# The first two tiles of x loaded turned, their means made on TensorE

## The chip, the cores and the metric

The kernel runs on one core of one Trainium2 chip. The metric is the device time of one execution in microseconds (us); the time of a kernel is the median of its runs.

## The reference

x is [1, 2048, 512] in fp32, 2048 tokens of 512 features. The output is a Fourier mixing of the normalized tokens, gated by an MLP on the same tokens, added to x:

```python
xn = _layernorm(x)                                   # over the 512 features, no weights
a  = einsum("bsd,ed->bse", xn, dft_hid_re)           # hidden DFT, 512 x 512
b  = einsum("bsd,ed->bse", xn, dft_hid_im)
s  = einsum("ts,bse->bte", dft_seq_re, a) - einsum("ts,bse->bte", dft_seq_im, b)
y  = _layernorm(xn)
h  = gelu(einsum("bsd,df->bsf", y, w1) + b1)         # 512 -> 1792
g  = silu(einsum("bsf,fd->bsd", h, w2) + b2)         # 1792 -> 512
out = x + s * g
```

## The kernel before

All products run on TensorE with fp32r operands: each fp32 operand is split into a rounded part (hi, an ACTIVATE copy on ScalarE) and the rest (lo, a subtraction on VectorE), and one product of whole values is taken as three: hi x hi, hi x lo and lo x hi. In `first_mm` a word such as "hl2" is one of these: the part of x, the part of the weight, and the feature chunk k of four.

The order of all instructions is written out by hand (`manual_schedule`); each engine runs its own in the order of the program and waits by semaphores. SP issues the loads in program order, and each waits for the landing of the eighth before it.

The hidden DFT comes first. Tokens are worked in tiles of 128, tiles 0 to 3 (the first 512 tokens) one by one. A product needs the feature axis on the partitions, for x as for the eight weight tiles W0 to W7 (four chunks k of the real matrix, m = 0, four of the imaginary, m = 1). `raw_w` are loaded by `load_w`, rounded by `round_w` (L356) and their rests made by `rest_w` (L81).

Tiles 2 and 3 are loaded twice: as rows (`x_load`, tile `x`), from which ScalarE makes minus the mean and the sum of squares (`first_mean`, `first_var`), and turned (`first_xT_load`, tile `xc`, features on the partitions). `first_transpose` brings the mean of each token to all partitions by one transpose (L311), VectorE adds it to the turned tile (L313), ScalarE rounds (L315), VectorE makes the rest (L316).

Tiles 0 and 1 are loaded as rows only. Tile 0's mean is made in two halves, one by ScalarE (L285), one by VectorE (L286, L287); VectorE centres the rows (L295), four transposes on TensorE turn them (L321), and two split steps per half tile (L62, L63) make hi and lo from PSUM. Tile 1 has its mean from ScalarE (L282), one centring (L291), four transposes and one split. Their squares are summed later on ScalarE from the centred tile (L302).

`idle_mm` issues products of a zero tile (L202) that nothing reads. `stats` makes mean and variance of tiles 4 to 7 on VectorE; `m_pack` (L171) packs their four means, `m_turn` (L179) turns them on TensorE. Tiles 4 to 7 are loaded turned, as one block of 512 tokens (`xt_load(1)`, L329), and centred at L334. `first_factors` (L141) makes the scale factors of tiles 0 to 7, by which ScalarE scales the products out of PSUM (`dft_out`, L431).

After this opening come the sequence DFT and the MLP, some 640 us of products, which the change doesn't touch.

Of the kernel before, what the change touches and what calls it, by code (L numbers as in the profile page):

```python
# [14 lines left out]
P = 128  # L15
# [5 lines left out]
def fnet_mixer_kernel(ctx: ExitStack, tc: tile.TileContext, x, xT, ct, wt, w1, w2, b1, b2, out):  # L21
# [118 lines left out]
    def first_factors():  # L140
        nc.vector.tensor_scalar(mv1[:, 2:NC, 1], mv1[:, 2:NC, 1], 1.0 / D, None, op0=ALU.mult)  # L141
        v = small.tile([P, 2 * HB], F32, tag="v", name="v")
        inner(v[:, :HB], mv1[:, :HB, 1], 1.0)
        outer(v[:, HB:], mv1[:, :HB, 1], 1.0)
        finish = rsqrt(rr[:, :2 * HB], v, 2 * HB)

        def both_signs():
            finish()
            nc.vector.tensor_scalar(nr1, rr[:, :HB], -1.0, None, op0=ALU.mult)

        return both_signs
# [52 lines left out]
    idle_mm(8)  # L204
# [10 lines left out]

    def parts(i):
        return 1 if i else 2
# [23 lines left out]
    x_load(0)  # L241
    for n in range(3):
        load_w(n)
    x_load(1)
    for n in range(3, 2 * NK):
        load_w(n)
    first_xT = {}

    def first_xT_load(i):
        first_xT[i] = plain(f"xc{i}").rearrange("p (k t) -> p k t", k=NK)  # L250
        nc.sync.dma_start(out=first_xT[i], in_=xT[TB[0], :, :, i * P:(i + 1) * P].rearrange("k p t -> p k t"))

    for i, load in ((4, x_load), (2, x_load), (5, x_load), (2, first_xT_load), (6, x_load), (3, x_load), (7, x_load),
                    (3, first_xT_load)):
        load(i)
# [6 lines left out]
    xc = {}  # L262

    half_means = [nr1[:, q:q + 1] for q in range(2)]
# [11 lines left out]
    def first_mean(i):  # L276
        if i > 1:
            nc.scalar.activation(junk(0), xs[i], AF.Copy, scale=-1.0 / D, accum_out=minus_mean(i))
            return
        xc[i] = plain(f"xc{i}")  # L280
        if i:
            nc.scalar.activation(xc[i], xs[i], AF.Copy, scale=1.0 / D, accum_out=mv1[:, i, 0:1])  # L282
            return
        n = D // 2
        nc.scalar.activation(xc[i][:, :n], xs[i][:, :n], AF.Copy, scale=1.0 / D, accum_out=half_means[0])  # L285
        nc.vector.reduce_sum(half_means[1], xs[i][:, n:], axis=mybir.AxisListType.X)  # L286
        nc.vector.tensor_scalar(half_means[1], half_means[1], 1.0 / D, None, op0=ALU.mult)  # L287

    def first_centre(i):
        if i:  # L290
            nc.vector.tensor_scalar(xc[i], xs[i], mv1[:, i, 0:1], None, op0=ALU.subtract)  # L291
            return
        n = D // 2
        for q in range(2):
            nc.vector.tensor_scalar(xc[i][:, q * n:(q + 1) * n], xs[i][:, q * n:(q + 1) * n], half_means[0],  # L295
                                    half_means[1], op0=ALU.subtract, op1=ALU.subtract)

    def first_var(i):
        if i > 1:
            nc.scalar.activation(junk(1), xs[i], AF.Square, bias=minus_mean(i), accum_out=mv1[:, i, 1:2])  # L300
            return
        nc.scalar.activation(xs[i], xc[i], AF.Square, scale=D ** -0.5, accum_out=mv1[:, i, 1:2])  # L302

    def first_transpose(i):
        t = operand(f"xt{i}")
        hi, lo = t[:, 0, :], t[:, 1, :]
        for k in range(NK):
            xt[i, k] = (hi[:, k * P:(k + 1) * P], lo[:, k * P:(k + 1) * P])
        if i > 1:
            pt = bank(f"pt{i}")  # L310
            nc.tensor.transpose(pt[:, :P], minus_mean(i).broadcast_to([P, P]), ident)  # L311
            c = first_xT[i]
            nc.vector.tensor_add(c, c, pt[:, None, :P].broadcast_to([P, NK, P]))  # L313
            c = c.rearrange("p k t -> p (k t)")
            nc.scalar.activation(hi, c, AF.Copy)  # L315
            return lambda: nc.vector.tensor_sub(lo, c, hi.bitcast(F32))  # L316
        n = D // parts(i)
        for q in range(parts(i)):
            pt = bank(f"pt{i}{q}")
            for k in range(NK // parts(i)):  # L320
                nc.tensor.transpose(pt[:, k * P:(k + 1) * P], xc[i][:, q * n + k * P:q * n + (k + 1) * P], ident)  # L321
            split_into(hi[:, q * n:(q + 1) * n], lo[:, q * n:(q + 1) * n], pt[:, :n])
# [125 lines left out]

    first_mean(0)
    first_centre(0)  # L450
    make_w(0)
    first_transpose(0)
    idle_mm(1)
    make_w(1, 2)
    first_mean(1)
    first_centre(1)
    make_w(3, 4)
    first_mm(0, 0, "hh0 hl0 lh0 hh1 lh1 hl1 hh2 lh2 hl2 hh3 lh3")
    first_transpose(1)
    first_mm(0, 0, "hl3")  # L460
    make_w(5, 6, 7)
    xt_load(1)
    for q in (12, 13, 8, 9):
        x_load(q)

    first_mm(0, 1, "hh0 lh0 hl0")
    first_mm(1, 0, "hh0 hl0 hh1 hl1 hh2 hl2 hh3 hl3 lh0 lh1 lh2 lh3")
    first_mean(2)
    first_var(0)
# [13 lines left out]
    nc.vector.tensor_add(mv1[:, 0, 0:1], *half_means)  # L483
# [225 lines left out]
    neg_means(0, 2)  # L709
# [690 lines left out]
```

## Time and profile before

| | us |
|---|---|
| median of 3 runs | 665.17 (664.75 to 665.47) |
| profiled execution | 665.25 |
| its span, first to last instruction | 663.5 |
| TensorE busy in the span | 658.4 |

The span begins with the first instruction and ends with the last; the 1.75 us of the profiled execution around it belong to its start and end. In rows, PE is TensorE's products, PEld its weight loads, ACT ScalarE, DVE VectorE, SP the engine that issues loads. "x4" merges four instructions that follow each other; the time given is then from the start of the first to the end of the last. A product's end lies behind the start of the next one, since products are pipelined: where the spacing of a series is wanted, the duration of one is to be taken off first. "idle before" says what the engine waited for.

### The profile page before, as it was taken

The numbers are of one execution on the slowest core, as the hardware profiler recorded it, in microseconds if no ns is written. First come the engines' busy times: TensorE is split into PE (matmuls) and PEld (weight loads), VectorE is DVE, ScalarE is ACT, GpSimd is POOL, SyncE is SP. The second block draws the span as 40 slices with busy tenths as digits, with TensorE's granted clock in tenths as the row PEclk, the third lists the DMA queues.
The fourth block names the chain that finished last, engine by engine and source line by source line (L and its number), as shares of the span: only waits on it lengthen the run. The fifth ranks groups of instructions, "written<-read, shape, count | busy, mean of one in ns | idle before, by whom it ended". The sixth has DMA issues, their size and how long they took to land.

```text
span 663.5 us, 8214 instructions
## 1 busy us (share of the span) xinstructions
PE 658.4 (99%) x2913; PEld 542.7 (82%) x2913; DVE 543.4 (82%) x584; ACT 361.0 (54%) x419; POOL 50.8 (8%) x84
## 2 busy tenths in 40 slices
PE   9999999999999999999999999999999999999997
PEld 5888888888888888888888888888888888888886
DVE  6899977877776866888979998739877299998986
ACT  6875567544446754555455544456444455746540
POOL 0002000321121100000000000000000001210100
PEclk9999999999999999999999999999999999999999
DMA  9979540987979999798699996416544558997984
GB/s 319 301 250 251 175 150 1 354 312 255 356 298 363 415 411 356 266 381 318 243 387 410 393 316 233 153 54 198 185 156 129 126 133 262 303 257 252 301 257 139
DMA packets 71869, 172.82 MB, mean 260 GB/s; under 512 B 6880, under 2 KB 22804, under 8 KB 71828
## 3 DMA queue, kind: packets, MB, share of 16 engines
q1 hardware_dynamic: 59488, 132.27, 56.9%
q0 software_dynamic: 12032, 39.86, 19.1%
q8 instruction: 23, 0.38, 0.2%
q10 hardware_dynamic: 308, 0.16, 0.1%
q14 instruction: 18, 0.15, 0.1%
HBM read 121.91 MB, written 50.36 MB: 260 GB/s over the span
## 4 chain that ended last, share of the span: by engine, by line
PE 99%; DMA 0%; DVE 0%; issue 0%; DVEq 0%
PE pz L1013 20%; PE px L1013 18%; PE ma L1013 11%; PE hy L828 11%; PE mb L1013 9%; PE hz L828 6%; PE pw L1013 5%; PE pd L408 3%; PE q1y L656 3%; PE hx L828 3%; PE pd L420 2%; PE px L1334 2%; PE pw L1334 2%; PE q1z L656 2%; PE quy L656 1%; PE q1x L656 1%
## 5 line engine op out<-in xcount | busy, mean ns | idle before, releaser
L1119 DVE TENSOR_TENSOR c<-c,c 128x1024 f32<-128x1024 f32 x32 | 39.1, 1222 | 3.4 <-DMA c<-ct 3.4
L81 DVE TENSOR_TENSOR w1l<-w1r,w1h 128x1792 fp32r<-128x1792 f32 x7 | 14.2, 2025 | 20.9 <-ACT w1h L527 20.9
L833 ACT ACTIVATE hc<-hc,b_t 128x1024 f32<-128x1024 f32 (+1 forms) x18 | 17.3, 962 | 25.1 <-DVE hc L873 22.6
L63 DVE TENSOR_TENSOR R_b1l<-c,R_b1h 128x1024 fp32r<-128x1024 f32 x16 | 19.5, 1221 | 13.0 <-ACT R_b1h L62 9.7
L62 ACT ACTIVATE R_s3h<-c 128x1024 fp32r<-128x1024 f32 x16 | 17.0, 1062 | 23.9 <-DVE c L1119 10.2
L1013 PE MATMUL pw<-R_s1h,L 128*128 128x512 f32 x96 | 29.7, 389 | 0.0
L62 ACT ACTIVATE R_b2h<-c 128x1024 fp32r<-128x1024 f32 x16 | 16.9, 1059 | 21.1 <-DVE c L1124 16.4
L63 DVE TENSOR_TENSOR R_s2l<-c,R_s2h 128x1024 fp32r<-128x1024 f32 x16 | 19.6, 1222 | 8.6 <-PE pz L1013 8.6
L62 ACT ACTIVATE R_s2h<-c 128x1024 fp32r<-128x1024 f32 x16 | 17.0, 1062 | 16.7 <-PE px L1013 9.3
L63 DVE TENSOR_TENSOR R_s3l<-c,R_s3h 128x1024 fp32r<-128x1024 f32 x16 | 19.6, 1224 | 3.9 <-PE pz L1013 3.8
L62 ACT ACTIVATE R_s1h<-c 128x1024 fp32r<-128x1024 f32 x16 | 16.4, 1052 | 11.3 <-DVE c L1130 11.3
L1127 POOL DMA_DIRECT2D c<-ct x8 | 7.0, 873 | 200.4 <-DVE c L1124 162.9
L62 ACT ACTIVATE R_b1h<-c 128x1024 fp32r<-128x1024 f32 x16 | 16.7, 1055 | 9.6 <-PE px L1013 4.4
L62 ACT ACTIVATE R_a1h<-c 128x1024 fp32r<-128x1024 f32 x16 | 16.9, 1055 | 8.9 <-PE pz L1013 7.2
L1013 PEld LDWEIGHTS pw<-R_s1h,L 128*128 128x128 f32 x96 | 18.0, 188 | 3.7
L63 DVE TENSOR_TENSOR R_b2l<-c,R_b2h 128x1024 fp32r<-128x1024 f32 x16 | 19.4, 1219 | 1.5 <-PE px L1013 1.5
L63 DVE TENSOR_TENSOR R_a1l<-c,R_a1h 128x1024 fp32r<-128x1024 f32 x16 | 19.5, 1221 | 1.3 <-PE px L1013 1.1
L63 DVE TENSOR_TENSOR R_s4l<-c,R_s4h 128x1024 fp32r<-128x1024 f32 x16 | 19.6, 1224 | 0.7 <-PE px L1013 0.7
L1124 DVE TENSOR_TENSOR c<-c,c 128x1024 f32<-128x1024 f32 x16 | 19.6, 1223 | 0.4
L62 ACT ACTIVATE R_s4h<-c 128x1024 fp32r<-128x1024 f32 x16 | 16.8, 1050 | 5.1 <-PE pz L1013 4.9
L63 DVE TENSOR_TENSOR R_s1l<-c,R_s1h 128x1024 fp32r<-128x1024 f32 x16 | 18.9, 1220 | 0.4 <-ACT R_s1h L62 0.2
L1013 PE MATMUL pw<-R_s1l,L 128*128 128x512 f32 x48 | 18.7, 389 | 0.0
(1000 smaller groups left out, 2221.4 us busy)
## 6 DMA issues: line engine op xcount, KB each, us to landing
c<-ct SPq DMA_DIRECT2D x68, 512.0 KB, 5.8
m<-h_d SPq DMA_DIRECT2D x48, 512.0 KB, 7.1
h_d<-ht POOLq DMA_DIRECT2D x21, 512.0 KB, 6.4
s_d<-sa SPq DMA_DIRECT2D x32, 256.0 KB, 3.7
la<-s_d SPq DMA_DIRECT2D x32, 256.0 KB, 5.7
h_d<-hc POOLq DMA_DIRECT2D x13, 512.0 KB, 3.7
x<-x SPq DMA_DIRECT2D x16, 256.0 KB, 5.6
sa<-a_d SPq DMA_DIRECT2D x8, 512.0 KB, 6.5
```

The source lines that it names most:

```text
L62: nc.scalar.activation(hi, src, AF.Copy)
L63: nc.vector.tensor_sub(lo, src, hi.bitcast(F32))
L81: nc.vector.tensor_sub(hi_lo[1], src, hi_lo[0].bitcast(F32))
L408: nc.tensor.matmul(acc, xt[i, k][px], weights[m * NK + k][pw], start=n == 0, stop=n == len(terms) - 1)
L420: nc.tensor.matmul(dacc[i, m], xt[i, k][px], weights[m * NK + k][pw], start=seen[i, m] == 0, stop=seen[i, m] == 3 * NK - 1)
L656: nc.tensor.matmul(qx[key], a, w, start=p in (1, 5, 2) and n == 0, stop=p in (2, 3, 4) and n == len(terms) - 1, skip_group_check=True)
L828: nc.tensor.matmul(acc[:, tau, :], w[:, W1_AT[p], k * P:(k + 1) * P], r[:, k, :], start=p in (1, 5, 2) and i == 0, stop=p in (2, 3, 4) and ...
L833: nc.scalar.activation(dst, src, AF.Gelu_apprx_tanh, bias=b1_t[:, row:row + 1])
L1013: nc.tensor.matmul(acc[k][:, tau, :], a, c[:, tau, :], start=first and i == 0, stop=last and i == len(terms) - 1, skip_group_check=True)
L1119: nc.vector.tensor_sub(t, t, raw)
L1124: nc.vector.tensor_add(raw, raw, t)
L1334: nc.tensor.matmul(acc[KEY[name]][k][:, tau, cols], a[k], c[:, tau, cols], start=False, stop=last and u == us[-1] and i == 2, skip_group_c ...
```

## The change

A new input `xf` holds the first 512 tokens turned, tile by tile (feature chunk, 128 tokens). Tiles 0 and 1 are loaded from it, in the places of SP's queue where their rows were loaded; the turned tiles 2 and 3 come from it too, in rows of 2 KB where there were four of 512 bytes. The mean of each token is made by TensorE: four fp32 products per tile with a matrix `per_d` whose values are all 1/512 sum a tile over its features and leave the mean in every partition. VectorE subtracts it, tile 0 in two halves and tile 1 in one, ScalarE rounds, VectorE makes the rests. The eight transposes of tiles 0 and 1 go, as do the sums that made their means. The rows of tiles 0 and 1 are loaded later, after those of tiles 4 and 2, and their means and squares are made from them on ScalarE, as for tiles 2 and 3. The idle products at the start are 5 and 2 in place of 8 and 1. Some orders change: the first products of tile 0 are split in two batches around tile 1's mean, tile 1's products come before the three of (0, 1), and the rows 12, 8 and 9 are loaded before the turned block of tiles 4 to 7.

```diff
@@ -138,7 +138,7 @@
         nc.vector.tensor_scalar(dst, var, scale * (1.0 + EPS), EPS * EPS, op0=ALU.mult, op1=ALU.add)
 
     def first_factors():
-        nc.vector.tensor_scalar(mv1[:, 2:NC, 1], mv1[:, 2:NC, 1], 1.0 / D, None, op0=ALU.mult)
+        nc.vector.tensor_scalar(mv1[:, :NC, 1], mv1[:, :NC, 1], 1.0 / D, None, op0=ALU.mult)
         v = small.tile([P, 2 * HB], F32, tag="v", name="v")
         inner(v[:, :HB], mv1[:, :HB, 1], 1.0)
         outer(v[:, HB:], mv1[:, :HB, 1], 1.0)
@@ -201,7 +201,10 @@
         for q in range(n):
             nc.tensor.matmul(idle_ps, idle[:, :P], idle, start=True, stop=True)
 
-    idle_mm(8)
+    per_d = consts.tile([P, P], F32, name="per_d")
+    nc.vector.memset(per_d, 1.0 / D)
+
+    idle_mm(5)
 
     xs = {}
 
...
@@ -238,20 +238,20 @@
     nc.scalar.activation(warm, warm, AF.Sqrt)
     nc.scalar.dma_start(out=touched[:P // 8].rearrange("p (n w) -> p n w", w=4),
                         in_=wt[:, :, 0:P:8, 0:4].rearrange("m k p w -> p (m k) w"))
-    x_load(0)
+    first_xT = {}
+
+    def first_xT_load(i):
+        first_xT[i] = plain(f"xc{i}").rearrange("p (k t) -> p k t", k=NK)
+        nc.sync.dma_start(out=first_xT[i], in_=xf[i])
+
+    first_xT_load(0)
     for n in range(3):
         load_w(n)
-    x_load(1)
+    first_xT_load(1)
     for n in range(3, 2 * NK):
         load_w(n)
-    first_xT = {}
-
-    def first_xT_load(i):
-        first_xT[i] = plain(f"xc{i}").rearrange("p (k t) -> p k t", k=NK)
-        nc.sync.dma_start(out=first_xT[i], in_=xT[TB[0], :, :, i * P:(i + 1) * P].rearrange("k p t -> p k t"))
-
-    for i, load in ((4, x_load), (2, x_load), (5, x_load), (2, first_xT_load), (6, x_load), (3, x_load), (7, x_load),
-                    (3, first_xT_load)):
+    for i, load in ((4, x_load), (2, x_load), (0, x_load), (1, x_load), (5, x_load), (2, first_xT_load), (6, x_load),
+                    (3, x_load), (7, x_load), (3, first_xT_load)):
         load(i)
     a_d = [dram.tile([2, P, D], F32, name=f"a_d{i}") for i in range(NS // 2)]
     b_d = [dram.tile([2, P, D], F32, name=f"b_d{i}") for i in range(NS // 2)]
...
@@ -274,52 +271,42 @@
         return nm[:, 2 * NC + i:2 * NC + i + 1]
 
     def first_mean(i):
...
+        nc.scalar.activation(junk(0), xs[i], AF.Copy, scale=-1.0 / D, accum_out=minus_mean(i))
 
     def first_var(i):
...
+        nc.scalar.activation(junk(1), xs[i], AF.Square, bias=minus_mean(i), accum_out=mv1[:, i, 1:2])
+
+    early_mean = {}
+
+    def mean_over(i):
+        early_mean[i] = bank(f"pm{i}")
+        for k in range(NK):
+            nc.tensor.matmul(early_mean[i][:, :P], per_d, first_xT[i][:, k, :], start=k == 0, stop=k == NK - 1)
+
+    def centre_first(i, ks):
+        c = first_xT[i][:, ks, :]
+        nc.vector.tensor_sub(c, c, early_mean[i][:, None, :P].broadcast_to([P, c.shape[1], P]))
+
+    first_op = {}
+
+    def first_round(i, ks):
+        if i not in first_op:
+            t = first_op[i] = operand(f"xt{i}").rearrange("p a (k t) -> p a k t", k=NK)
+            for k in range(NK):
+                xt[i, k] = (t[:, 0, k, :], t[:, 1, k, :])
+        nc.scalar.activation(first_op[i][:, 0, ks, :], first_xT[i][:, ks, :], AF.Copy)
+
+    def first_rest(i, ks):
+        hi, lo = (first_op[i][:, q, ks, :] for q in range(2))
+        nc.vector.tensor_sub(lo, first_xT[i][:, ks, :], hi.bitcast(F32))
 
     def first_transpose(i):
...
+        pt = bank(f"pt{i}")
+        nc.tensor.transpose(pt[:, :P], minus_mean(i).broadcast_to([P, P]), ident)
+        c = first_xT[i]
+        nc.vector.tensor_add(c, c, pt[:, None, :P].broadcast_to([P, NK, P]))
+        first_round(i, slice(0, NK))
+        return lambda: first_rest(i, slice(0, NK))
@@ -446,27 +433,43 @@
             round_w(n)
             rest_w(n)
 
+    front, back, whole = slice(0, 2), slice(2, NK), slice(0, NK)
+    mean_over(0)
+    idle_mm(2)
+    centre_first(0, front)
+    centre_first(0, back)
+    round_w(0)
+    first_round(0, front)
+    round_w(1)
+    first_round(0, back)
+    round_w(2)
+    first_rest(0, front)
+    rest_w(0)
+    first_rest(0, back)
+    rest_w(1)
+    rest_w(2)
+    first_mm(0, 0, "hh0 lh0 hh1 lh1 hl0")
+    mean_over(1)
+    centre_first(1, whole)
+    round_w(3)
+    round_w(4)
+    first_round(1, whole)
+    rest_w(3)
+    first_rest(1, whole)
+    rest_w(4)
+    first_mm(0, 0, "hh2 lh2 hl1 hh3 lh3 hl2 hl3")
+    make_w(5, 6, 7)
+    for q in (12, 8, 9):
+        x_load(q)
+    xt_load(1)
+    x_load(13)
+
+    first_mm(1, 0, "hh0 hl0 hh1 hl1 hh2 hl2 hh3 hl3 lh0 lh1 lh2 lh3")
+    first_mm(0, 1, "hh0 lh0 hl0")
+    first_mean(2)
     first_mean(0)
-    first_centre(0)
-    make_w(0)
-    first_transpose(0)
-    idle_mm(1)
-    make_w(1, 2)
+    first_var(0)
     first_mean(1)
-    first_centre(1)
-    make_w(3, 4)
-    first_mm(0, 0, "hh0 hl0 lh0 hh1 lh1 hl1 hh2 lh2 hl2 hh3 lh3")
-    first_transpose(1)
-    first_mm(0, 0, "hl3")
-    make_w(5, 6, 7)
-    xt_load(1)
-    for q in (12, 13, 8, 9):
-        x_load(q)
-
-    first_mm(0, 1, "hh0 lh0 hl0")
-    first_mm(1, 0, "hh0 hl0 hh1 hl1 hh2 hl2 hh3 hl3 lh0 lh1 lh2 lh3")
-    first_mean(2)
-    first_var(0)
     first_var(1)
     stats(mv1, xs[NC], NC)
     stats(mv1, xs[NC + 1], NC + 1)
@@ -480,7 +483,6 @@
     rest_2()
     stats(mv1, xs[NC + 3], NC + 3)
     m_pack()
-    nc.vector.tensor_add(mv1[:, 0, 0:1], *half_means)
     first_mm(1, 1, "hh0 hh1 hh2 hh3 lh0 lh1 lh2 lh3 hl0 hl1 hl2 hl3")
 
     def means_out():
@@ -706,7 +708,6 @@
     for q in (10, 11):
         stats(mv1, xs[q], q)
     neg_means(2)
-    neg_means(0, 2)
     a_sum(7)
     dft_mm(3, 0)
     dft_mm(3, 1)
@@ -1381,6 +1382,7 @@
     arrays = {
         "x": a["A_x"][0],
         "xT": a["A_x"][0].T.reshape(D // P, P, S // W, W).transpose(2, 0, 1, 3),
+        "xf": a["A_x"][0, :W].T.reshape(D // P, P, W // P, P).transpose(2, 1, 0, 3),
         "ct": np.stack([seq_halves(a["A_dft_seq_re"]), seq_halves(a["A_dft_seq_im"])]),
         "wt": np.stack([a[n].T.reshape(D // P, P, D) for n in ("A_dft_hid_re", "A_dft_hid_im")]),
         "w1": a["B_w1"].reshape(2, 2, P, 2, F // P // 2, P).transpose(4, 2, 3, 0, 1, 5).reshape(
```

## Rows read from the trace of the kernel before

**Rows 1.** The page, part 1: busy us, share of the span, instructions.

```profile
PE 658.4 (99%) x2913; PEld 542.7 (82%) x2913; DVE 543.4 (82%) x584; ACT 361.0 (54%) x419; POOL 50.8 (8%) x84
```

**Rows 2.** Chain of waits in order of time: start us, us, what.

```profile
0.75 2.93 DMA x<-x
...
4.98 1.09 PE pt L321 x4
6.06 0.43 PE idle_ps L202
6.49 2.97 PE pd L420 x11
9.89 5.06 PE pd L420 x22
...
72.01 16.32 PE q1y L656 x72
```

**Rows 3.** Timeline, all engines, 14 to 25 us: start, us, what, [idle before].

```profile
14.80 0.27 PE L311 MATMUL pt<-ident,fm 128*128 128x128 f32 x1
...
18.05 0.17 DVE L171 COPY rsm<-mv 128x4 f32<-128x4 f32 x1
...
18.33 0.08 PEld L179 LDWEIGHTS rpm<-ident,rsm 128*4 128x4 f32 x1 [0.24 <-issue]
...
24.50 2.35 DVE L334 TENSOR_TENSOR xT<-xT,rowm 128x1024 f32<-128x1024 f32 x2
```

**Rows 4.** Timeline of PE, 0 to 12 us.

```profile
1.20 3.60 PE L202 MATMUL idle_ps<-idle 128*128 128x512 bf16 x8 [1.20 <-DVE warm L237]
4.98 1.09 PE L321 MATMUL pt<-ident,xc 128*128 128x128 f32 x4 [0.18 <-DVE xc L295]
5.86 0.63 PE L202 MATMUL idle_ps<-idle 128*128 128x512 bf16 x1
6.11 3.35 PE L420 MATMUL pd<-W,xt 128*128 128x512 f32 x11
9.30 0.60 PE L321 MATMUL pt<-ident,xc 128*128 128x128 f32 x4
```

**Rows 5.** Two windows: busy us by engine, PEclk, DMA share, GB/s.

```profile
4.50:5.00 0.50, 0.32 (x2) 0.05 (x1) 0.50 (x2) 0.50 (x1) 0.00 (x0) 1.00 1.04 389
...
9.00:10.00 1.00, 1.00 (x8) 0.82 (x8) 0.99 (x2) 0.26 (x2) 0.00 (x0) 1.00 0.99 369
```

**Rows 6.** Loads issued at 2.62, 3.09, 7.67, 11.70 us: size, us to landing.

```profile
x<-x SPq DMA_DIRECT2D x1, 256.0 KB, 4.4
...
rw<-wt SPq DMA_DIRECT2D x1, 256.0 KB, 4.6
...
xc<-xT SPq DMA_DIRECT2D x1, 256.0 KB, 5.6
...
xT<-xT SPq DMA_DIRECT2D x1, 512.0 KB, 7.2
```

**Rows 7.** Timeline of PE near the end: first and last of seven products.

```profile
658.11 0.28 PE L1334 MATMUL px<-R_b1l,L 128*128 128x224 f32 x1
...
658.77 0.28 PE L1334 MATMUL px<-R_b1l,L 128*128 128x224 f32 x1
```

**Rows 8.** Timeline of ScalarE (ACT) and VectorE (DVE), 3.5 to 8 us.

```profile
5.67 0.81 ACT L62 ACTIVATE xt<-pt 128x256 fp32r<-128x256 f32 x2 [0.62 <-PE pt L321]
6.09 0.85 DVE L63 TENSOR_TENSOR xt<-pt,xt 128x256 fp32r<-128x256 f32 x2 [0.31 <-ACT xt L62]
6.38 1.14 ACT L356 ACTIVATE W<-rw 128x512 fp32r<-128x512 f32 x2
...
7.04 1.29 DVE L81 TENSOR_TENSOR W<-rw,W 128x512 fp32r<-128x512 f32 x2
```

**Rows 9.** Timeline of VectorE and ScalarE, 12 to 16 us.

```profile
15.10 0.69 DVE L313 TENSOR_TENSOR xc<-xc,pt 128x512 f32<-128x512 f32 x1 [0.43 <-PE pt L311]
...
15.83 0.63 ACT L315 ACTIVATE xt<-xc 128x512 fp32r<-128x512 f32 x1 [1.90 <-DVE xc L313]
```

More of the change, by code (lines that the diff above doesn't have):

```diff
@@ L20, in fnet_mixer_kernel @@
 @with_exitstack
-def fnet_mixer_kernel(ctx: ExitStack, tc: tile.TileContext, x, xT, ct, wt, w1, w2, b1, b2, out):
+def fnet_mixer_kernel(ctx: ExitStack, tc: tile.TileContext, x, xT, xf, ct, wt, w1, w2, b1, b2, out):
     nc = tc.nc
@@ L213, in tok @@
         return TB[i // NC] * NC + i % NC
-    def parts(i):
-        return 1 if i else 2
     def x_load(i):
@@ L240, in fnet_mixer_kernel @@
                         in_=wt[:, :, 0:P:8, 0:4].rearrange("m k p w -> p (m k) w"))
-    x_load(0)
-    for n in range(3):
-        load_w(n)
-    x_load(1)
-    for n in range(3, 2 * NK):
-        load_w(n)
     first_xT = {}
@@ L250, in first_xT_load @@
         first_xT[i] = plain(f"xc{i}").rearrange("p (k t) -> p k t", k=NK)
-        nc.sync.dma_start(out=first_xT[i], in_=xT[TB[0], :, :, i * P:(i + 1) * P].rearrange("k p t -> p k t"))
-    for i, load in ((4, x_load), (2, x_load), (5, x_load), (2, first_xT_load), (6, x_load), (3, x_load), (7, x_load),
-                    (3, first_xT_load)):
+        nc.sync.dma_start(out=first_xT[i], in_=xf[i])
+    first_xT_load(0)
+    for n in range(3):
+        load_w(n)
+    first_xT_load(1)
+    for n in range(3, 2 * NK):
+        load_w(n)
+    for i, load in ((4, x_load), (2, x_load), (0, x_load), (1, x_load), (5, x_load), (2, first_xT_load), (6, x_load),
+                    (3, x_load), (7, x_load), (3, first_xT_load)):
         load(i)
@@ L261, in fnet_mixer_kernel @@
     xt = {}
-    xc = {}
-    half_means = [nr1[:, q:q + 1] for q in range(2)]
     squares = []
@@ L276, in first_mean @@
     def first_mean(i):
[L277 to L296, printed above, removed]
-    def first_var(i):
[L299 to L302, printed above, removed]
@@ L304, in first_transpose @@
-    def first_transpose(i):
[L305 to L322, printed above, removed]
+        nc.scalar.activation(junk(0), xs[i], AF.Copy, scale=-1.0 / D, accum_out=minus_mean(i))
```

## The prediction, made before the changed kernel ran

> **What bounds the kernel now.** The page's first part comes first: TensorE (PE) is busy for 99% of the span [rows 1], so a change shows in the time only if it lengthens or shortens PE's own stream. The chain of waits says where that stream isn't yet closed: it runs through a load, VectorE and TensorE up to about 15 us, and from there through products that stand 0.227 us apart (72 in 16.32 us) with nothing between them [rows 2]. The change lies wholly in that opening. The point to watch is the transpose for tile 2, which starts at 14.80 [rows 3] after 4 + 4 transposes and 33 products: from there on the two kernels issue the same products in the same order, so the change is worth the shift of that one instruction, plus whatever arrives late behind it.
>
> The opening has two levels of speed. Four transposes of 128 columns take 1.09 us at 4.98, and the same four 0.60 us at 9.30; with the durations of the last one taken off (0.42, 0.27) they stand 0.22 and 0.11 us apart. Eight idle products of 512 columns stand 0.43 us apart, later ones 0.23 [rows 2, 4]. The granted clock reads 1.00 in both stretches [rows 5], but the spacings say that TensorE ran at 1.2 GHz until a little after 6 us and at 2.4 GHz from then on. The first mean falls in the slow part, the second in the fast one.
>
> **The change, part by part.** *Loads.* The first turned tile takes the place of the first row tile in SP's queue, with the same 256 KB, and lands at 0.75 + 2.93 = 3.68 [rows 2]. The second lands where row tile 1 did, at 2.62 + 4.4 = 7.0 [rows 6]. The early weights keep their places, and with them their landings (weight 3 at 3.09 + 4.6 = 7.7, weight 5 at 8.9).
>
> *Price of one fp32 product.* No row shows one. The lower end is the transpose of the same shape, 0.22 us at the slow level and 0.11 at the fast one. What bounds that row is probably its weights, for products of 224 columns stand just as far apart (seven starts, six intervals in 0.66 us: 0.11) [rows 7]: 128 or 224 columns, the spacing doesn't change. The upper end is a 512-column product with a load of weights that nothing hides: 0.43 + 0.22 = 0.65, at the fast level 0.34. I take 0.43 and 0.23, the rows of the 512-column product, the nearest to the middle between the ends. One pass over 128 columns is not likely to be all: for whole fp32 values the kernel itself takes three products of rounded parts (hh, hl, lh).
>
> *Tile 0.* Five idle products end their issue at 1.20 + 5 x 0.43 = 3.35, before the load lands. Products start at 3.72, the last at 3.72 + 3 x 0.43 = 5.01, its result at 5.64, 0.63 later, as long as the idle product at 5.86 takes [rows 4]. VectorE centres the front half in 0.42 (half-tile subtractions, 0.85 for two with overlap) [rows 8], 5.68 to 6.10. ScalarE, which has rounded weight 0 at 4.42 as before, rounds it in 0.38 [rows 8], 6.13 to 6.51. The two idle products end at 6.3 and cost nothing: behind them PE waits anyway. First weights at 6.56, and with 0.11 for that load the first product at 6.67; before it was 6.11 [rows 4]. This step costs 0.56: reduction, centring, transposes and rounding (3.68 to 6.06) give way to products, centring and rounding (3.68 to 6.51).
>
> *From there to the transpose of tile 2.* ScalarE: weight 1 6.41 to 7.03, back half to 7.32, weights 2, 3, 4 to 7.84, 8.36 and 8.93 (0.62 each, 0.52 apart: two in 1.14) [rows 8]. VectorE: back half centred by 6.45; rests of front half to 6.97, weight 0 to 7.58, back half to 7.92, weight 1 to 8.53, weight 2 to 9.14 (0.69 each, 0.60 apart, halves 0.42). PE: hh0 to 6.90; lh0 waits for 6.97 and runs 7.14 to 7.37; hh1, lh1, hl0 to 8.06; the second mean, 4 x 0.23, to 8.98, its result at 9.15; six products to 10.36. Meanwhile VectorE centres tile 1 from 9.19 to 9.88 (0.69, the row of a 512-element subtraction with a PSUM operand) [rows 9]; the rest of weight 3 is queued behind it and ends at 10.49, and ScalarE rounds tile 1 by 10.54. So the last product of that batch, hl3, stalls: 10.66 to 10.89. Then 12 + 3 + 6 products without a wait (rest of tile 1 at 11.3, of weight 4 at 11.9, weights 5 to 7 rounded at 11.1 to 12.1): 21 x 0.227 = 4.76, and the transpose starts at 15.65 against 14.80.
>
> As a sum: first product +0.56; second mean 0.92 in place of four transposes 0.44, +0.48; stalls now 14.80 - 6.11 - 33 x 0.227 - 0.44 = 0.76, then 0.58, -0.18. Together **+0.86 us**.
>
> *What is moved behind it.* The rows of tiles 0 and 1 come after those of 4 and 2, 0.5 MB in front of all later loads; at 0.66 us per 256 KB (weight 3 to weight 5: 7.7 to 8.9, two loads) each later landing moves by 1.3 us: the turned tile 2 from 7.67 + 5.6 = 13.3 to 14.6 [rows 6], needed at 15.97. The turned block for tiles 4 to 7 also has three row tiles in front of it now (12, 8, 9): it lands 1.3 + 2.0 us later than its 11.7 + 7.2 = 18.9 [rows 6], at 22.2, and is wanted at 24.50 + 0.86 [rows 3]. ScalarE gets two more sums of 0.62 + 0.19 us, in a stretch in which it sat idle for 1.90 us [rows 9]: from 12.0 on its three sums and two variances end at 12.0 + 0.61 + 2 x 1.46 = 15.5, before the rounding of tile 2 at 16.7. Tiles 2 and 3 turned come in rows of 2 KB, which can only help their landings. VectorE loses the half-tile reduction and three one-column operations. The narrowest point is the packing of four means at 18.05, whose transpose loads weights at 18.33 [rows 3]: VectorE's rests end some 0.6 us later than before, its packing at 19.1, PE gets there at 19.2. All this I cost at nothing; with the cover gone, PE would stand by the amount the packing is late.
>
> **Forecast.** The profiled execution took 665.25 us (span 663.5 and 1.75 around it), the median is 665.17, 0.08 less. 665.17 + 0.86 = **666.0 us**, within the 0.2% (1.3 us) that a measurement of this kernel can tell.
>
> **Rivals.** *Weights not hidden (slower).* If each fp32 product waits for its own weights, 0.65 and 0.34 apart, the first mean ends 0.66 + 0.2 later and the second 0.44 later: 0.86 + 0.86 + 0.3 to 0.44 = +2.1, **667.3**. For it: 128-column work is bound by weights already [rows 7]. Against: the 512-column rows hide the load entirely. It turns the verdict from a spacing of about 0.53 on at the slow level.
>
> *As cheap as a transpose.* At 0.22 and 0.11 the first mean is there at 4.8, the first product at 5.7, still at the slow level; then weight 3, which lands at 7.7, and VectorE's rests set the pace. Second mean 0.44, transpose of tile 2 at 14.7: -0.1, **665.1**. For it: shape and operand type are the same. Against: a transpose only moves values, and the kernel's own way to a product of whole values costs three.
>
> *A product as dear as four transposes.* 0.87 and 0.44 apart: three products by 6.33, the fourth at the fast level, result near 6.9 (+1.3), second mean 1.76 (+0.84): +3.0, **668.2**. For it: nothing in the trace sets a ceiling. Against: 0.87 is twice the row of a product with four times the columns. The Trainium skill, TensorE: Matmul & The Clock Gate, section Terms, says that the transpose mode is four times as fast for FP32; by that rule a product would cost four of the transposes in the trace, and the sum would be this one. No row of this trace shows it or speaks of it, since none has such a product.
>
> *The moved loads bite.* If the 0.5 MB delays tiles 6 and 7 by 1 us more than worked out, the packing is late and PE stands: **667.0**. Against: each landing above has at least 1 us to spare.
>
> **How the numbers follow.** Forecast 0.56; weights not hidden 0.20; cheap as a transpose 0.10; as dear as four transposes 0.07; loads 0.04; anything better 0.03, for PE has 7.5 us of products to do after about 5.6 whatever the means cost, so that a gain over 1.1 us isn't to be had in this opening. Faster by over 0.2%: 0.04 (the tails of the forecast and of the cheap case, and the unknown). Slower by over 0.2%, above 666.5: 0.18 + 0.07 + 0.02 of the rivals and 0.07 of the forecast, 0.34. Within: 0.62. Range 664.6 to 667.6: the cheap case below, weights not hidden above, the four transposes left out.
>
> **What would show it.** In the trace after: four fp32 products 0.43 apart from 3.7 and 0.23 apart near 8; first product of the transform at 6.6 to 6.7; one short stall before hl3; transpose of tile 2 near 15.65; the packing no later than PE's arrival; no gap in PE from there on. Wrong is the forecast if the products' spacing lies elsewhere, if the clock rises at another time, or if PE stands between 15 and 36 us.

## The result, and the profile after

The changed kernel takes 666.66 us (median of 18 runs, 666.31 to 667.56), the one before 665.15 (18 runs, 664.75 to 666.11): a ratio of 1.0022 [1.0016, 1.0029], 1.51 us slower. The forecast was 666.0 in a range of 664.6 to 667.6, so the range holds it; of the shift, 0.86 was forecast and 1.51 came, which is just past the bound of 0.2%. The profiled execution took 666.7, with a span of 664.9 (+1.45 against before's profile).

The page, part 1, of the kernel after, as in [rows 1]:

```profile
PE 658.9 (99%) x2919; PEld 543.5 (82%) x2919; DVE 542.7 (82%) x581; ACT 362.3 (54%) x419; POOL 50.7 (8%) x84
```

PE has 6 records more than before. Eight transposes and two idle products went; if each of the eight fp32 products were one record, there would be 2 fewer. Each is two, with two loads of weights.

The timeline of PE in the kernel after, 0 to 16.2 us (start us, us, what, [idle before]), where [rows 4] and the first row of [rows 3] stood:

```profile
1.19 2.32 PE L202 MATMUL idle_ps<-idle 128*128 128x512 bf16 x5 [1.19 <-DVE idle L197]
3.65 1.67 PE L284 MATMUL pm<-xc,per_d 128*128 128x128 f32 x8
5.16 0.59 PE L202 MATMUL idle_ps<-idle 128*128 128x512 bf16 x2
6.28 1.94 PE L407 MATMUL pd<-W,xt 128*128 128x512 f32 x5 [0.53 <-ACT xt L297]
8.06 1.05 PE L284 MATMUL pm<-xc,per_d 128*128 128x128 f32 x8
8.87 6.91 PE L407 MATMUL pd<-W,xt 128*128 128x512 f32 x28
15.62 0.27 PE L305 MATMUL pt<-ident,fm 128*128 128x128 f32 x1
```

The first product stands at 6.28 (6.11 before), the second mean takes 0.81 (8.06 to 8.87), and the transpose of tile 2 stands at 15.62 against 14.80. Behind the first of them, the single records of the first mean stand 0.213 us apart up to 4.64, from 4.83 on 0.111; those of the second mean 0.111. So TensorE went from 1.2 to 2.4 GHz at about 4.8, while it was still in the first mean; before, it did so a little after 6.

What VectorE does in the kernel after, 4 to 12 us:

```profile
5.36 0.75 DVE L288 TENSOR_TENSOR xc<-xc,pm 128x256 f32<-128x256 f32 x2 [4.08 <-PE pm L284]
6.26 0.43 DVE L301 TENSOR_TENSOR xt<-xc,xt 128x256 fp32r<-128x256 f32 x1 [0.15 <-ACT xt L297]
6.61 0.68 DVE L81 TENSOR_TENSOR W<-rw,W 128x512 fp32r<-128x512 f32 x1
7.55 0.42 DVE L301 TENSOR_TENSOR xt<-xc,xt 128x256 fp32r<-128x256 f32 x1 [0.26 <-ACT xt L297]
7.89 1.28 DVE L81 TENSOR_TENSOR W<-rw,W 128x512 fp32r<-128x512 f32 x2
9.15 0.69 DVE L288 TENSOR_TENSOR xc<-xc,pm 128x512 f32<-128x512 f32 x1
9.76 0.68 DVE L81 TENSOR_TENSOR W<-rw,W 128x512 fp32r<-128x512 f32 x1
10.54 0.69 DVE L301 TENSOR_TENSOR xt<-xc,xt 128x512 fp32r<-128x512 f32 x1
11.15 2.49 DVE L81 TENSOR_TENSOR W<-rw,W 128x512 fp32r<-128x512 f32 x4
```

VectorE sits idle until the first mean is there, for 4.08 us, and from 7.89 on has no idle time that counts. Tile 1's mean is complete at 9.12 (last record 8.84 + 0.28), when VectorE comes out of weight 2's rest at 9.17: the mean and the queue arrive together.

Further on, the round trip of the four turned means in the kernel after, all engines, 18 to 37 us (ACTq and SPq are DMA issues):

```profile
18.88 0.17 DVE L171 COPY rsm<-mv 128x4 f32<-128x4 f32 x1
...
19.19 0.27 PE L179 MATMUL rpm<-ident,rsm 128*4 128x128 f32 x1
...
19.80 0.50 ACTq L183 DMA_DIRECT2D rdm<-rtm  x1
...
22.69 0.93 SPq L357 DMA_DIRECT2D rowm<-rdm  x2
...
25.92 2.36 DVE L321 TENSOR_TENSOR xT<-xT,rowm 128x1024 f32<-128x1024 f32 x2 [0.50 <-DMA rowm<-rdm]
...
35.73 0.18 DVE L129 SCALAR_TENSOR_TENSOR fm<-tv,y 128x16 f32<-128x16 f32 x1
...
36.05 0.27 PE L179 MATMUL rpR<-ident,fm 128*36 128x128 f32 x1
```

and in the kernel before, for the rows of it that are not in [rows 3]:

```profile
18.36 0.27 PE L179 MATMUL rpm<-ident,rsm 128*4 128x128 f32 x1
...
18.96 0.50 ACTq L183 DMA_DIRECT2D rdm<-rtm  x1
...
21.19 0.81 SPq L370 DMA_DIRECT2D rowm<-rdm  x2
...
34.31 0.18 DVE L129 SCALAR_TENSOR_TENSOR fm<-tv,y 128x16 f32<-128x16 f32 x1
...
35.18 0.27 PE L179 MATMUL rpR<-ident,fm 128*36 128x128 f32 x1
```

The means are written to memory (rdm) and read back, one copy to each partition (rowm); the read is issued when the write has landed. That took 21.19 - 18.96 = 2.2 us before and 2.9 after. From rpm to rpR, the transpose of the scale factors, PE has 35.18 - 18.36 = 16.82 and 36.05 - 19.19 = 16.86: a difference of 0.04, so PE hardly waits in either. But VectorE's centring now waits 0.50 for the row (before, for nothing). From its start to the start of the last step that makes the factors (L129) it is 9.81 us in both kernels, 24.50 [rows 3] to 34.31 and 25.92 to 35.73, and 35.73 is 0.32 ahead of rpR. In two runs below in which PE does wait at rpR, it is 0.32 as well, so that is the least. The kernel before has 0.87 there, 0.55 to spare; after the change nothing is left.

The delay goes through to the end: first q1y at 51.00 (50.09), last product of PE at 660.49 (659.56, +0.93). Behind that, 0.5 us more are lost. The records of SP at the end, start us and the two semaphores waited for (the first of the two, from 101 to 110, is that of a DMA); the last store was issued at 660.71 before and 661.64 after:

```
before                        after
661.842  108, 100             662.078  118, 116
662.524  109, 102             663.601  101, 115
662.586  110, 103             663.665  103, 114
662.651  drain                ...      (105 to 109, 0.06 each)
...                           664.028  110, 104
663.417                       664.095  drain
                              ...
                              664.865
```

SP waits for the DMAs' semaphores one after the other, in a fixed order, 0.06 us each. The last store carries semaphore 109 before, the last but one, and 101 after, the first of the eight: seven waits now stand behind its landing instead of one. In all: PE +0.93, landing of the last store 1.96 against 1.81, +0.15, waits behind it +0.37; the sum is the +1.45 of the span.

### The profile page after: what moved, and what is told of

It reads as the page before. It is cut to its first block, busy times and chain, and to the rows that moved or that the text cites. A ratio compares the mean times of both kernels' runs of the same rounds, so it can differ in the third digit from the quotient of the medians.

```text
span 664.9 us, 8223 instructions
## 1 busy us (share of the span) xinstructions
PE 658.9 (99%) x2919; PEld 543.5 (82%) x2919; DVE 542.7 (82%) x581; ACT 362.3 (54%) x419; POOL 50.7 (8%) x84
## 4 chain that ended last, share of the span: by engine, by line
PE 99%; DMA 0%; DVE 0%; ACT 0%; issue 0%
PE pz L1014 20%; PE px L1014 18%; PE hy L829 11%; PE ma L1014 11%; PE mb L1014 9%; PE hz L829 6%; PE pw L1014 5%; PE pd L395 3%; PE q1y L658 3%; PE hx L829 3%; PE pd L407 2%; PE px L1335 2%; PE pw L1335 2%; PE q1z L658 2%; PE quy L658 1%; PE q1x L658 1%
## 5 line engine op out<-in xcount | busy, mean ns | idle before, releaser
L62 ACT ACTIVATE w2h<-w 128x1024 fp32r<-128x1024 f32 (+1 forms) x14 | 13.2, 946 | 11.4 <-DVE w L942 3.9
```

The source lines that it names most:

```text
L62: nc.scalar.activation(hi, src, AF.Copy)
```

## The experiments

Theory A puts the loss on PE's own stream, as the prediction summed it: the second mean's 0.9 us of products can't be hidden. Theory B puts it on what feeds PE: VectorE's queue in the opening, and later the round trip of the means. The ending is separate from both. A gate is below a point at which PE has to stop when something that it needs comes late. Each kernel has one profiled execution, and executions of the same text differ in the opening by some tenths of a us, so one trace shows a mechanism and seldom a price.

**The ending.** Loads of 128 bytes, issued between 388 and 454 us, far from both ends, move the last store to another semaphore: two in the kernel before, seven in the kernel after.

```diff
+        if u in (8, 12):
+            nc.sync.dma_start(out=touched[0:1, :], in_=x[0:1, 0:W // 16])
```

> The kernel before, with two loads of 128 bytes that nothing reads, issued by SP far from both ends (about 430 us). The ending waits for the landings of the eight store and load slots one after the other, in a fixed order; before, the slot of the last store is the seventh of the eight, after the change it is the first, because two more loads were issued. Theory (the order of those waits costs time): the two small loads turn the slots in the same way, TensorE's stream stays where it was, and the span grows by 0.4 to 0.5 us: about 665.6. Rival (the tail of the changed kernel is longer only because its last store happened to land late, or because of the 0.5 MB more): no change, 665.15.

665.71 us, ratio 1.0007 [0.9998, 1.0016]. The last store carries 101, and 1.32 us pass from its landing to the end (0.96 before): +0.36 in the trace, +0.58 between the medians, where the interval goes from -0.1 to +1.1. The trace shows something else, far ahead of the small loads. The opening was earlier than in the profile of the kernel before (transpose of tile 2 at 14.37, not 14.80), and yet PE's last product came 0.24 later (659.80, not 659.56). The timelines of VectorE, 35 to 50 us, and PE, 33 to 52 us, in this run:

```profile
45.39 1.23 DVE L544 TENSOR_TENSOR xT<-xT,rowR 128x1024 f32<-128x1024 f32 x1 [1.00 <-DMA rowR<-rdR]
...
48.90 0.70 PE L656 MATMUL quy<-W,uh 128*128 128x512 f32 x2 [0.46 <-DVE qu L644]
```

The scale factors make the same round trip as the means (rdR, rowR). Here their row came late, and the wait of VectorE reached PE. So the kernel before has a gate at 48.9 us already, at which an early opening can lose what it gained.

```diff
+        if u in (8, 10, 12, 14, 16, 18, 20):
+            nc.sync.dma_start(out=touched[0:1, :], in_=x[0:1, 0:W // 16])
```

> The changed kernel with seven such loads of 128 bytes between about 430 and 445 us, so that the last store falls on the eighth slot, the last that is waited for. Theory: seven waits of 0.06 us no longer stand behind the last landing: 0.4 us less, about 666.2, with TensorE's last product where it is. Rival (late landing by chance, or more bytes): no change, 666.66.

665.98 us, 1.0012 [1.0004, 1.0021]. Semaphore 110, 0.89 us from landing to end against 1.33: 0.44 of the 0.68 by which it is faster than the kernel after are in the ending. The rest, 0.24, is less than the interval can tell. In its profiled execution the transpose of tile 2 stood at 15.15, not 15.62, though the text up to there is the same.

**Is the second mean on the path?** First it was left out, with its PSUM bank:

```diff
-    mean_over(1)
+    early_mean[1] = early_mean[0]
```

> The changed kernel without the second mean: tile 1 is centred by tile 0's mean, so the four fp32 products near 8 us are left out. Theory A (TensorE's own sum bounds the opening): all of their 0.89 us comes back, about 665.8. Theory B (VectorE's queue bounds it: it has no idle time from the first centring to the last rest of a weight): VectorE gets to tile 1 only 0.06 us earlier, and hl3 waits for the rest of weight 3 as before: 0.05 to 0.15 less, about 666.6.

667.6 us, 1.0035 [1.0021, 1.0049], slower than the kernel after: neither theory. PE's weight loads in this kernel, waits from 60 to 92 us (who waited for whom: us in total, times, longest):

```profile
PEld hy L829 <- ACT q L641: 1.2, 1, 1.2
```

Which of the eight PSUM banks a tile gets depends on the tiles before it. The build gives the last tile of q1y bank 2 in the kernels before and after, and bank 1 in this one; the first hy takes banks 0 and 1. So PE stands at 88.7 while ScalarE is still emptying q1y, 0.9 us beyond the usual spacing of two products. The next kernel takes the bank and leaves out the products only (one 128-column bf16 product in place of eight records):

```diff
-    mean_over(1)
+    early_mean[1] = early_mean[0]
+    pm1 = bank("pm1")
+    nc.tensor.matmul(pm1[:, :P], idle[:, :P], idle[:, :P], start=True, stop=True)
```

> The changed kernel without the second mean, as in the earlier run (tile 1 is centred by tile 0's mean, the four fp32 products are left out), but with the PSUM bank of that mean still taken, by one 128-column bf16 product. In the earlier run the banks had moved on by one, and near 88.7 us a product of the MLP waited 0.95 us for ScalarE to empty its bank. Theory B (VectorE's queue sets the pace behind the first centring): that wait is gone, the transpose of tile 2 moves by less than 0.2 us against the changed kernel for the same first product, 666.4 to 666.7. Theory A (TensorE's own sum): 665.8.

666.61 us, 1.0022 [1.0013, 1.0030], the same as with the mean. The 665.8 of Theory A lies below the interval. The timeline of its PE, 5 to 16 us:

```profile
6.08 1.65 PE L407 MATMUL pd<-W,xt 128*128 128x512 f32 x5 [0.53 <-ACT xt L297]
7.57 0.23 PE L454 MATMUL pm<-idle 128*128 128x128 bf16 x1
7.61 1.67 PE L407 MATMUL pd<-W,xt 128*128 128x512 f32 x6
9.88 5.30 PE L407 MATMUL pd<-W,xt 128*128 128x512 f32 x22 [0.60 <-DVE W L81]
15.01 0.27 PE L305 MATMUL pt<-ident,fm 128*128 128x128 f32 x1
```

PE reaches hl3 earlier and waits 0.60 there for weight 3's rest. From the first product to the transpose of tile 2 it is 8.93; in the two traces that have the mean and the same text otherwise, 15.15 - 6.09 = 9.06 (seven loads) and 15.62 - 6.28 = 9.34 (the kernel after). So 0.8 us of products are worth 0.1 to 0.4 here: nearer to Theory B for the opening.

**VectorE's queue.** The rest of weight 0 ahead of the centring, which fills part of VectorE's idle 4 us:

```diff
+    round_w(0)
+    rest_w(0)
     centre_first(0, front)
...
-    round_w(0)
...
-    rest_w(0)
```

> The changed kernel with the rest of weight 0 ahead of the centring of tile 0 on VectorE, at 4.95 us, where VectorE waits for the mean in any case until 5.36. Theory B (VectorE's queue bounds the opening): the first centring starts 0.2 us later, but all that follows on VectorE ends 0.4 us earlier, and hl3 with it: 0.2 to 0.4 less, about 666.35. Theory A (TensorE's sum, begun by the first product): first product 0.2 later, 666.85.

666.55 us, 1.0022 [1.0013, 1.0031]: no change that can be told, and between the two expectations. In its profiled execution the spacing of PE's records changed only at 7.37, and the first product stood at 6.66, so the trace doesn't compare with the kernel after's. Two products of (0, 1) ahead of hl3, so that PE has work while the rest is made:

```diff
-    first_mm(0, 0, "hh2 lh2 hl1 hh3 lh3 hl2 hl3")
+    first_mm(0, 0, "hh2 lh2 hl1 hh3 lh3 hl2")
+    seen[1, 0], dacc[1, 0] = 0, bank("pd1_0")
+    first_mm(0, 1, "hh0 lh0")
+    first_mm(0, 0, "hl3")
...
-    first_mm(0, 1, "hh0 lh0 hl0")
+    first_mm(0, 1, "hl0")
```

> The changed kernel with one reordering on TensorE: two products that need no rest of a weight (hh0 and lh0 of the pair (0, 1), with weight 4) stand ahead of hl3, which waits for the rest of weight 3. Theory B (VectorE's queue sets the pace, and TensorE waits for it at lh0 and at hl3): the 0.3 to 0.7 us of waiting at hl3 are filled, as far as tile 1's rounding lets TensorE go on at about 10.5: transpose of tile 2 0.2 to 0.4 earlier for the same first product, 666.35. Rival (the wait only moves to the next product, hh0 of tile 1): no change, 666.66.

666.5 us, 1.0020 [1.0010, 1.0029]. The wait at hl3 is gone and first product to transpose of tile 2 fell to 15.24 - 6.50 = 8.74 (9.34 and 9.06 with the order of the kernel after); the medians don't tell it from the kernel after. The same rest on GpSimd:

```diff
+    nc.gpsimd.tensor_sub(weights[0][1], raw_w[0], weights[0][0].bitcast(F32))
...
-    rest_w(0)
```

> The changed kernel with the rest of weight 0 made by GpSimd, which is idle there, in place of VectorE. Theory B: VectorE has 0.60 us less in its queue ahead of tile 1's centring, so that the second mean on TensorE becomes the later of the two; hl3 and the transpose of tile 2 come 0.2 to 0.4 earlier, 666.35, if GpSimd is done before hl0 wants its result at about 7.6 (the subtraction starts at 4.9). Theory A (TensorE's sum): no change, 666.66. Rival (GpSimd needs over 2.7 us or slows VectorE): slower than 666.7.

666.4 us, 1.0025 [1.0015, 1.0035]. In the trace the transpose of tile 2 is 0.56 earlier, at 15.06. That isn't the edit's work: the first product already stands at 6.01 (the turned tile 0 landed at 3.28, in the kernel after at 3.52), and from there it is 9.05, as with seven loads (9.06). But the trace shows that most of an early opening is given back. Its PE, 14 to 37 us:

```profile
15.06 0.27 PE L305 MATMUL pt<-ident,fm 128*128 128x128 f32 x1
...
34.28 1.29 PE L395 MATMUL pd<-W,xt1h 128*128 128x512 f32 x5
35.88 0.27 PE L179 MATMUL rpR<-ident,fm 128*36 128x128 f32 x1 [0.31 <-DVE fm L129]
```

The transpose rpR stands 0.17 earlier than after's 36.05, not 0.56: PE got there in time and waited for the factors. The two starts on either side of the wait are 698 ns apart, 0.47 more than the 0.227 of a product. This is a second gate, and the row's round trip in this run was 3.6 us. The last two edits and the seven loads together:

```diff
+    nc.gpsimd.tensor_sub(weights[0][1], raw_w[0], weights[0][0].bitcast(F32))
...
+    first_mm(0, 1, "hh0 lh0")
+    first_mm(0, 0, "hl3")
...
+        if u in (8, 10, 12, 14, 16, 18, 20):
+            nc.sync.dma_start(out=touched[0:1, :], in_=x[0:1, 0:W // 16])
```

> The changed kernel with the rest of weight 0 on GpSimd, the two products ahead of hl3, and seven small loads that put the last store on the eighth slot: everything of these runs that could give the changed kernel back its time. 0.4 from the ending, 0.3 to 0.6 from the opening: 665.6 to 665.9, still above the 665.1 of the kernel before, as the first product comes no earlier and the second mean stays on TensorE.

665.78 us, 1.0013 [1.0004, 1.0022], as expected; the seven loads alone gave 665.98, from which it can't be told apart. The transpose of tile 2 is at 14.96, and PE waits some 0.2 at rpR.

**Tile by tile.** Only tile 0 turned, tile 1 as rows again; then only tile 1 turned. Both have the ending of before.

```diff
-    first_xT_load(1)
+    x_load(1)
...
-    mean_over(1)
-    centre_first(1, whole)
...
+    first_mean(1)
+    centre_rows()
+    make_w(3, 4)
+    first_mm(0, 0, "hh2 lh2 hl1 hh3 lh3 hl2")
+    turn_rows()
+    first_mm(0, 0, "hl3")
```

> Half of the change: tile 0 is loaded turned with its mean by fp32 products; tile 1 is loaded as rows, its mean by ScalarE, four transposes, as in the kernel before. Seven small loads put the last store back on the slot it has in the kernel before, so that the ending is the same and only the opening differs. Theory B: the first product is 0.2 to 0.5 later, tile 1 costs VectorE 0.2 less than the turned way; +0.2 to +0.5 against before: 665.5. Theory A: +0.2 to 0.5 too, as the second mean is gone: 665.5. Rival (the second mean does all the harm or the first does): 665.1 or 666.0.

666.39 us, 1.0015 [1.0006, 1.0024], 0.9 more than expected. PE in it, 9 to 12 us:

```profile
10.07 0.48 PE L421 MATMUL pd<-W,xt 128*128 128x512 f32 x1
11.00 1.19 PE L421 MATMUL pd<-W,xt 128*128 128x512 f32 x4 [0.45 <-ACT xt L62]
```

The order, taken from the kernel after, puts tile 1's products right behind its transposes, and PE waits for their rounding. So this kernel doesn't give the price of turning tile 0 alone.

```diff
-    first_xT_load(0)
+    x_load(0)
...
-    mean_over(0)
-    idle_mm(2)
-    centre_first(0, front)
-    centre_first(0, back)
...
+    centre_rows()
+    make_w(0)
+    turn_rows()
+    idle_mm(1)
+    make_w(1, 2)
```

> The other half: tile 0 as rows as before, tile 1 loaded turned with its mean by fp32 products; again with seven small loads for the same ending. The second mean's 0.89 us stands on TensorE in place of 0.44 of transposes. Theory A (TensorE's sum): +0.45: 665.6. Theory B (VectorE's queue): tile 1's centring takes 0.69 in place of 0.48 and comes after the mean; +0.2 to +0.4: 665.4. Both halves together should come to the opening's +0.8 to +0.9, if the two parts add.

666.98 us, 1.0025 [1.0014, 1.0036], 1.4 to 1.6 more than expected. Its order of tiles puts the last q1y in bank 1 again, with as many tiles as in the kernel before, and PE stands 0.93 us at 88.6, before the same hy as above. The halves of the change don't add up, and neither of these two tells what one costs.

**The moved loads alone.** The kernel before, with two row tiles (256 KB each) loaded where the change puts tiles 0 and 1, into a tile that nothing reads, and six small loads that keep the last store on 109:

```diff
+    more = guest("more")
+
+    def more_load(q):
+        nc.sync.dma_start(out=more[:, q, :], in_=x[q * P:(q + 1) * P, :])
+
-    for i, load in ((4, x_load), (2, x_load), (5, x_load), (2, first_xT_load), (6, x_load), (3, x_load), (7, x_load),
-                    (3, first_xT_load)):
+    for i, load in ((4, x_load), (2, x_load), (0, more_load), (1, more_load), (5, x_load), (2, first_xT_load),
+                    (6, x_load), (3, x_load), (7, x_load), (3, first_xT_load)):
...
+        if u in (8, 10, 12, 14, 16, 18):
+            nc.sync.dma_start(out=touched[0:1, :], in_=x[0:1, 0:W // 16])
```

> The kernel before with the moved loads alone: two row tiles (256 KB each) that nothing reads are loaded where the change loads the rows of tiles 0 and 1, and six small loads late in the kernel keep the last store on its slot. Theory (the moved loads use up the cover of a later point: TensorE's transpose of the factors near 35 us, which in the changed kernels follows the turning of the four means by 16.0 to 16.9 us of waits, while TensorE itself needs 16.5): the chain from the means to the factors grows from 15.95 by 0.2 to 0.8 us, TensorE waits there by 0 to 0.3: 665.1 to 665.4. Rival (the moved loads are wholly hidden): chain as before, 665.1. Rival (they delay tiles 6 and 7 and with them the four means): 665.6 or more, with a wait at about 18.4.

666.09 us, 1.0014 [1.0005, 1.0023]: 0.94 slower than before, more than either expectation. All engines, 17 to 37 us:

```profile
18.05 0.27 PE L179 MATMUL rpm<-ident,rsm 128*4 128x128 f32 x1
...
18.65 0.50 ACTq L183 DMA_DIRECT2D rdm<-rtm  x1
...
23.10 0.81 SPq L375 DMA_DIRECT2D rowm<-rdm  x2
...
25.95 2.36 DVE L339 TENSOR_TENSOR xT<-xT,rowm 128x1024 f32<-128x1024 f32 x2 [0.75 <-DMA rowm<-rdm]
...
35.75 0.17 DVE L129 SCALAR_TENSOR_TENSOR fm<-tv,y 128x16 f32<-128x16 f32 x1
36.07 0.27 PE L179 MATMUL rpR<-ident,fm 128*36 128x128 f32 x1 [1.05 <-DVE fm L129]
```

Its opening is faster than before's (rpm at 18.05, not 18.36), and still rpR stands at 36.07, where the kernel after has it (36.05). The write of 8 KB issued at 18.65 took 4.45 us until the read could be issued, 2.2 before. What the DMA engines moved says why: between 21.0 and 21.5 nothing before, but 385 GB/s here (389 in the kernel after), and here they moved data until 22.5. In all three the write landed when the loads in front of it had all but run out. From the centring on it is 9.80 and 0.32 again. PE stood idle for 1.05 us, and its starts on either side are 1.44 apart.

The counter-test is the kernel of the last two edits and the small loads, without the row loads of tiles 0 and 1:

```diff
-    for i, load in ((4, x_load), (2, x_load), (0, x_load), (1, x_load), (5, x_load), (2, first_xT_load), (6, x_load),
+    for i, load in ((4, x_load), (2, x_load), (5, x_load), (2, first_xT_load), (6, x_load),
...
+    xs[0], xs[1] = xs[2], xs[4]
...
+        if u in (6, 7, 8, 10, 12, 14, 16, 18, 20):
+            nc.sync.dma_start(out=touched[0:1, :], in_=x[0:1, 0:W // 16])
```

> The last version (rest of weight 0 on GpSimd, two products ahead of hl3, last store on the eighth slot) without the loads of the rows of tiles 0 and 1: their means and squares are taken from the rows of tiles 2 and 4, so the output is not the reference's; two more small loads keep the slot. Theory: the wait of 0.2 us before the transpose of the factors near 35.2 is gone: 665.4 to 665.65 against 665.78. Rival (that chain does not depend on these loads): no change, 665.78.

665.82 us, 1.0010 [1.0001, 1.0019]: no faster than with the loads (665.78, +0.75 against its own before, here +0.67), so the expectation fell. In the trace the gate is open again: 2.6 us for the round trip, rpm to the factors 15.93 (15.95 before, 16.54 after), and no wait at rpR. But the profiled execution's opening is as late as the kernel after's, transpose of tile 2 at 15.65, with the change of spacing at 7.7 and the first product at 6.66; with the loads it was 4.7, 6.17 and 14.96. So in this execution one gate was taken away, and the late opening took its place. It was the slowest of the 11 (665.99); why their median is no lower, its trace can't say.

Taken together, against the kernel before: the moved loads alone cost 0.94 us (0.3 to 1.5), the turned opening alone, in its last version, 0.67 (0.1 to 1.3), the two in that version 0.75 (0.3 to 1.5), and in the kernel after with its ending put right 0.85 (0.3 to 1.4). The prices don't add up. The traces give a reason, that a late opening hides the late row at rpR and the other way round; with intervals this wide it remains a reading.

No kernel of these is faster than the one before.

## Why the prediction was right, and where it was wrong

*The opening's sum held, term by term less well.* The transpose of tile 2 stood at 15.62, forecast 15.65. That it fits to 0.03 is luck in part: the same text gave 15.15 in the run with seven loads, and the kernel before's own 14.80 was 14.37 with two small loads. The price of a product was right, though it was picked between two far ends and no row showed it, which is luck too. A product of whole fp32 values costs 0.427 and 0.223 us (two records of 0.213 and 0.111) for the forecast 0.43 and 0.23, and its own weights are hidden or part of that, so "weights not hidden" and "as dear as four transposes" are out, and so is "cheap as a transpose": it costs two. The Trainium skill, TensorE: Matmul & The Clock Gate, section Terms, gives the transpose mode as four times as fast for FP32; the trace has 0.223 against 0.111, a factor of 2. The Trainium skill, FP8 and Floating Point Precision, section TensorE Precision Notes, counts four passes for a true FP32 product; four passes of 128 columns are 512 columns, for which this trace has 0.227 (an estimate from that page's count). The trace's 0.223 agrees, though it shows two records and not the passes.

*The clock rose earlier than assumed, and a load came later.* The first product was due at 6.67, since the slow level was taken to last past 6; it came at 6.28. By the prediction's own sign (the clock rises at another time) that step was wrong. In three other executions, with the first mean begun at 3.65 as here, the slow level did last through it, and there the first product stood at 6.66. What was gained was lost again: ScalarE got weight 1 at 6.58 (forecast 6.41) and weight 3 at 8.55 (it was to land at 7.7), and the second mean began at 8.06, the forecast time. These two cancelled by chance, and both move from one execution to the next: the spacing changed anywhere between 4.4 and 7.7 us in these traces, the first product in the kernels with both tiles turned stood between 6.01 and 6.66.

*The sum named the wrong owner.* The prediction gave +0.48 of the loss to the second mean on PE. Without these products the kernel took the same time: in the trace PE waited for the rests on VectorE instead, and then some 0.2 for the factors. A sum along PE gave the right time because VectorE's queue ended beside it.

*The step that failed: "All this I cost at nothing", of the moved loads.* It looked at the packing, which held as forecast (18.88, PE there at 19.19), and at the landing of the turned block. It didn't follow the means to the block's other operand, the row that goes out to memory and back behind the same bulk loads. Alone, the moved loads cost 0.94 us. In the trace of the kernel after they cost PE 0.04 on top, since the opening is late by about as much: rpR is at 36.07 with one cause and at 36.05 with the other. The rival "the moved loads bite" had about the right size, 1 us, and the wrong place.

*The term that was missing: the ending.* Two more loads on the queues than before moved the last store to the first of the semaphores that SP waits for: +0.37 in the trace, +0.36 and -0.44 in the two tests of it. With it, +0.93 and +0.15 make the span's +1.45. The forecast of +0.86 is thus PE's part, 0.93 in this execution, and the rest is what it didn't look at.

*What would show it.* No gap of PE from the transpose of tile 2 on: right in the kernel after, but with no slack left at 36 us. Of the five kernels that had an earlier opening and the moved loads, three waited there (0.2, 0.5 and 0.2 us), and two didn't.

Executions with the same text on PE differ by up to 0.7 us at the transpose of tile 2 (14.96 and 15.65 in the last version). The traces show two sources: when the loads land (the first one between 3.28 and 3.52 with both tiles turned, 3.21 and 3.67 with neither) and when the clock rises. Still open: what moves these two; what part of the opening costs its time; what one turned tile alone costs; and whether the three edits of the opening's order are worth anything by themselves, which intervals of about 0.6 us to either side don't tell.

## What to carry to other kernels

Follow each moved load to the small transfers that run behind it, and ask for the slack of the last operand to arrive, not only of the one that was moved: here a write of 8 KB landed only when the bulk loads in front of it had all but run out. Where two gates lie in a row, a delay at one can hide the other, so that taking away either shows nothing; price each alone, on the kernel before. A change in the number of loads, or in the number or order of PSUM tiles, can have a price of its own, at the end or at a bank, that has nothing to do with what they are for: keep them when a part is tested. And profile a kernel more than once before a difference of some tenths of a us in its opening is put down to an edit.

## What the runs showed of the hardware

- An fp32 product of 128 x 128 by 128 columns is two records on PE, 0.213 us apart at 1.2 GHz and 0.111 at 2.4; a transpose of the same shape is one.
- The change from 1.2 to 2.4 GHz came between 4.4 and 7.7 us in executions whose starts hardly differ, while the granted clock read 1.00 on either side of it [rows 5], and from 1 to 8 us in the kernel after and in the last version without the rows.
- A write of 8 KB took 2.2 (before) to 4.45 us until its landing let the next DMA issue. It landed when the loads issued ahead of it had all but run out: at about 21.2 before, 22.7 in the kernel after, 23.1 with the moved loads alone. With the same loads ahead it took 2.2 us in one execution and 2.9 in another.
- From the landing of the last store to the end it is 0.89, 0.96 or 1.33 us, by which semaphore the store carries.
- One PSUM tile fewer in the opening cost 0.9 us of PE at 88.7, some 80 us later, where a product's bank was still being emptied; two tiles in another order did the same.
